# First pair's low halves by TensorE and ScalarE, and its maxima's turn and two scores placed ahead of the second pair's join and maxima

## The chip, the cores and the metric

The kernel runs on one core of one Trainium2 chip. Its time is device time in microseconds (us), median of the runs shown. The engines of the core work side by side, each through its own instructions in a fixed order: TensorE (PE in the profile; its weight loads are PEld), VectorE (DVE), ScalarE (ACT), GpSimd (POOL) and SyncE (SP), which issues all transfers of this kernel.

## The reference, cut to what matters

Attention with rotary positions, then a soft mixture of experts on its output:

```python
q_rot, k_rot = rotate(q), rotate(k)              # 8 batches, 8 heads, 576 positions, 64 wide
scores = (q_rot @ k_rot.T) / 8
attn = softmax(scores)                           # with the row's maximum taken off
x = (attn @ v) as 4608 x 512
logits = x @ phi                                 # 32 slots
d = softmax of logits over the 4608 rows;  c = softmax of logits over the 32 slots
slots = d.T @ x;  slots = relu(slots @ w1[e]) @ w2[e]   # 8 experts, 4 slots each
out = c @ slots
```

## The kernel before, in words

Heads are worked in 32 pairs, two heads a pair, one on each half of the 128 partitions. For a pair, q and k (`t` = 0 and 1) are loaded with their rotated partners (`load0`, `load1`), multiplied with cosine and sine (`spin0`, `spin1`, on POOL but for pair 0, which DVE does at the start), and added (`join`, DVE). The float32 result is then split: `high` (ACT) rounds it to fp16, and `low` (DVE, line 254) takes that off the float32 value and keeps the rest as fp16. So `halves[p]` holds four fp16 rows of 576: QL, QH, KH, KL. `low` is also the last reader of the loaded tile. There are two such tiles (`x_in`), so the load of pair p + 2 waits for `low` of pair p.

For the maxima of the scores there are eight units `m00` to `m31` (line 287) and `m_rem`: TensorE multiplies high halves, and DVE reduces the result to maxima. For pair 0, all units from the fourth on carry two extra matmuls that only keep TensorE at work (line 293). `m_min` joins the nine results. For pairs 0 and 1, `m_rows` is `m_lay` (line 343): float32 matmuls with the identity turn the maxima, and ACT writes them as fp16 to `peaks[p % 2]`. A score `t0` to `t8` (lines 360 and 376) is the sum of three products of halves and of a product with the peaks, and ACT takes its exponent from PSUM. `av0` to `av4` multiply with the values.

PSUM is cut in four buffers (`ps0` to `ps3`). `bank2()` gives the buffer that was freed longest ago, in the order of the program, or a named one, `bank2(k)`. A buffer has one copy: whoever gets it waits until every reader of the tile before has finished, also a reader that stands later in the program. `FIRST` turns the order in which the buffers are first given. Units, scores and turns take one buffer each in rotation; the accumulator of `av` keeps one from `av0` until it has been read.

PE, ACT and DVE each follow the order of the program. For the first part that order is the hand-written list `FRONT` (lines 87 to 110): names with pair numbers, such as `m11.0`. After it the events follow by due times. `heat` (line 720) issues matmuls whose result nobody reads. `id_sb`, the identity, is loaded at line 751, behind both loads of pair 1 and ahead of the values of pair 0. SP and POOL follow program order too.

After the last pair's `av4` (lines 787 to 802) the end of the attention runs: `natural` turns the outputs of pairs 29, 30 and 28 with nine transposes each (line 480), in named buffers; `norm_last` (line 458) lets DVE divide pair 31's accumulator straight from PSUM (lines 463 to 471); `natural_out` (line 500) copies the turned outputs by ACT; `natural_last` turns and copies pair 31; the logits of the last batch (line 506) take all four.

```python
    others = release_att()
    natural(last - 2, 2)
    natural(last - 1, 1)
    natural(last - 3, 0)
    norm_last(last)
    ...
    lt = bank2(2)
    ...                       # natural_last takes bank2(1) and bank2(3)
```

Then come the two layers of the experts (lines 903 and 927) and the combination (line 950) with the stores of the output.

Of the kernel before, what the change touches and what calls it, by code (L numbers as in the profile page):

```python
# [11 lines left out]
ALU = mybir.AluOpType  # L12
# [14 lines left out]
HC = S // 2  # L27
# [57 lines left out]
    3.879855, 5.365764), "bs3": 34.500363, "bs4": 35.968859, "bs5": 43.198227, "bs6": 50.043832,  # L85
}
FRONT = (
# [70 lines left out]
def attn_softmoe(ctx, tc, qk, v, phi, w1, w2, cs, ident, sel, seg, out):  # L158
    nc = tc.nc
    P = 128  # L160
# [23 lines left out]
    id_sb = const.tile([P, P], F32, name="id_sb")  # L184
# [9 lines left out]
    peaks = [const.tile([P, S], F16, name=f"peak{i}") for i in range(2)]  # L194
# [16 lines left out]
    loaded = {}  # L211
    halves = {}
    half = (slice(0, HC), slice(HC, S))
    parts = [slice(i, i + 1) for i in range(PIECE)]
    halves_q = (slice(0, PIECE // 2), slice(PIECE // 2, PIECE))
# [5 lines left out]
    def cut4(x):  # L221
        return x.rearrange("p (q w) -> p q w", w=PW)
# [23 lines left out]
    def high(p, t, c=every):  # L246
        if p not in halves:
            halves[p] = stk.tile([P, 4, S], F16, name="hl")
        out = cut4(halves[p][:, 1 + t, PW * c.start:PW * c.stop])
        nc.scalar.copy(out=out, in_=loaded[p][:, t, c, 0])  # L250

    def low(p):
        x, hl = loaded.pop(p), halves[p].rearrange("p t (q w) -> p t q w", w=PW)
        nc.vector.tensor_tensor(out=hl[:, 0:4:3], in0=x[:, :, :, 0], in1=hl[:, 1:3], op=ALU.subtract)  # L254
# [13 lines left out]
    def bank2(k=None):  # L268
        if k is None:
            k = min((i for i in range(N_S) if age[i] is not None), key=lambda i: age[i])  # L270
        age[k] = None
        t = ps[k].tile([P, 2, 512], F32, name=f"s_ps{k}")
        held[id(t)] = k, t
        return t

    def free(t):
        k, _ = held.pop(id(t))
        age[k] = next(ages)
# [397 lines left out]
    def part(k):  # L676
# [13 lines left out]
        "spin1": lambda p: spin(p, 1, nc.gpsimd, parts),  # L690
        "join": join,
        "high0": lambda p: high(p, 0),
        "high1": lambda p: high(p, 1),
        "low": low,
        "m_rem": m_rem,
# [24 lines left out]
    def heat(n):  # L720
        cold = bank2()
        free(cold)
        for _ in range(n):
            nc.tensor.matmul(cold[:, 0, 0:HC], lhsT=lift, rhs=halves[0][:, KH, 0:HC], start=True, stop=True)  # L724

    def small_loads(p):
# [1 line left out]
        nc.sync.dma_start(out=sel_sb, in_=sel)  # L728

    plan.update({  # L730
        "heat": lambda p: heat(16),
        "small_loads": small_loads,
        "join0": lambda p: join(p, 0),
        "join1": lambda p: join(p, 1),
# [1 line left out]
    done = set()  # L736
# [7 lines left out]
    for t, cc in ((1, 0), (1, 1), (0, 0), (0, 1)):  # L744
        c = halves_q[cc]
# [7 lines left out]
    for t in (1, 0):  # L753
        for c in halves_q:
            spin(0, t, nc.vector, (c,))
            join(0, t, c)
            high(0, t, c)
    done.update((n, 0) for n in ("spin0", "spin1", "join", "high0", "high1", "load0", "load1"))
    done.update((n, 1) for n in ("join0", "join1"))
    heat(N_WARM)  # L760

    last = NPAIR - 1
# [89 lines left out]
    for c in range(2):  # L852
        for j in range(4):
            nc.tensor.matmul(sh[c][32 * j:32 * j + 32], lhsT=dn[:, 32 * j:32 * j + 32],
                             rhs=xn[:, j, 256 * c:256 * c + 256], start=True, stop=True, tile_position=(0, 32 * j))
    for i in range(NP):
        nc.tensor.matmul(rp[32 * i:32 * i + 32], lhsT=dn[0:64, P + 32 * i:P + 32 * i + 32],
                         rhs=xn[0:64, 4, i * P:(i + 1) * P], start=True, stop=True, tile_position=(0, 32 * i))
# [31 lines left out]
    for _ in range(N_LEAD):  # L890
        load_w(wp, N_W)
    nc.vector.tensor_tensor(out=st[:, 0:256].rearrange("p (i e z) -> p i e z", i=NP, z=2 * SPE)[:, :, :, SPE:],
                            in0=fp[:, 0:P].rearrange("p (i e z) -> p i e z", i=NP, z=SPE),
# [173 lines left out]
```

## Time and profile before

| | us |
|---|---|
| median of 3 runs | 479.99 (479.64 to 480.94) |
| the profiled execution | 480.02 |
| its span | 478.2 |

| engine | busy us | share of the span |
|---|---|---|
| PE | 458.3 | 96% |
| PEld | 371.5 | 78% |
| DVE | 366.3 | 77% |
| POOL | 288.0 | 60% |
| ACT | 285.7 | 60% |

All times in the rows below are microseconds from the start of the span. A row of a timeline has start, length, engine, line of the kernel, operation, what it writes and reads, and in brackets how long the engine stood idle before it and what ended that. Consecutive instructions of one kind are merged in one row (x5). "PEclk" is the share of TensorE's full clock (2.4 GHz) that was granted; 0.50 is the other level, 1.2 GHz. 1.8 us of the execution lie outside the span.

### The profile page before, as it was taken

To read this page: it belongs to the slowest core of one execution; us is meant where nothing else is said; L and a number is where in the kernel's file an instruction comes from. 1 tells how busy PE (TensorE), PEld (TensorE's weight loads), DVE (VectorE), ACT (ScalarE), POOL (GpSimd) and SP (SyncE) were. 2 spreads that over 40 slices of the span, in tenths; PEclk is the share of its full clock that TensorE was granted. 3 is DMA by queue.
4 is the path that set the end of the run, shared out by engine and by line. 5 is a ranking of instruction groups with operands and counts; after the bars stand their busy time and mean duration, and the time that the engine had idled before them with its cause. 6 is when DMAs were issued, how large, how long until landed. Compare 5 with 4: busy or idle time off the path is not lost.

```text
span 478.2 us, 24158 instructions
## 1 busy us (share of the span) xinstructions
PE 458.3 (96%) x10787; PEld 371.5 (78%) x10787; DVE 366.3 (77%) x616; ACT 285.7 (60%) x656; POOL 288.0 (60%) x319
## 2 busy tenths in 40 slices
PE   4799999999999999999999999999999999989993
PEld 2487888878888888878887888888888888853762
DVE  5989998888878887998899789988896864263242
ACT  2156767675667567657765676577766766530242
POOL 4886958848783888488856886687749302120000
PEclk9899999999999999999999999999999999999998
DMA  7444845473655355446533653346352044799997
GB/s 280 172 166 176 269 153 197 164 261 102 202 175 213 110 201 174 120 145 210 171 113 123 250 172 125 149 139 217 126 191 112 15 181 163 237 382 407 408 370 319
DMA packets 28795, 93.97 MB, mean 196 GB/s; under 512 B 5012, under 2 KB 5396, under 8 KB 28692
## 3 DMA queue, kind: packets, MB, share of 16 engines
q1 hardware_dynamic: 28692, 92.44, 54.1%
q8 instruction: 84, 1.38, 1.2%
q14 instruction: 19, 0.16, 0.1%
HBM read 82.92 MB, written 9.44 MB: 193 GB/s over the span
## 4 chain that ended last, share of the span: by engine, by line
PE 91%; DVE 4%; ACT 2%; DMA 1%; issue 1%; SPq 0%; DVEq 0%; ACTq 0%
PE s_ps L407 33%; PE s_ps L372 26%; PE s_ps L296 8%; PE s_ps L387 4%; PE o_ps L927 3%; PE o_ps L903 3%; PE s_ps L480 2%; PE s_ps L517 2%; PE c_ps L950 2%; DVE nm L298 2%; PE s_ps L724 2%; PE s_ps L305 2%; PE s_ps L577 1%; DVE hl L254 1%; DMA x_in<-in_qk 1%
## 5 line engine op out<-in xcount | busy, mean ns | idle before, releaser
L237 POOL TENSOR_TENSOR x_in<-x_in,cs_sb 128x288 f32<-128x288 f32 x248 | 236.2, 986 | 79.5 <-DMA x_in<-in_qk 62.5
L298 DVE TENSOR_REDUCE nm<-s_ps 128x2 f32<-128x576 f32 x256 | 187.3, 752 | 50.0 <-PE s_ps L296 48.8
L407 PEld LDWEIGHTS s_ps<-v_in,a_t 128*64 128x64 f32 x4608 | 139.3, 137 | 12.4 <-issue 4.8
L373 ACT ACTIVATE a_t<-s_ps 128x576 f32<-128x576 f32 x256 | 146.0, 658 | 3.6 <-PE s_ps L372 3.1
L407 PE MATMUL s_ps<-v_in,a_t 128*64 128x66 f32 x4608 | 146.4, 222 | 0.2 <-issue 0.2
L372 PE MATMUL s_ps<-hl 64*128 64x288 f16 x1536 | 133.1, 283 | 0.4 <-DVE nm L307 0.2
L372 PEld LDWEIGHTS <-hl 64*128 64x128 f16 x1536 | 79.3, 94 | 18.5 <-issue 8.0
L372 PE MATMUL s_ps<-peak,lift 64*128 64x288 f16 x512 | 75.3, 283 | 0.3 <-ACT peak L349 0.3
L296 PE MATMUL s_ps<-hl 64*128 64x288 f16 x512 | 66.8, 286 | 0.7 <-ACT a_t L373 0.4
L438 ACT COPY o_sb<-s_ps 128x528 f32<-128x528 f32 x31 | 18.6, 601 | 74.9 <-PE s_ps L407 74.9
L456 POOL TENSOR_TENSOR xn<-o_sb,rr 128x640 f32<-128x640 f32 x31 | 41.0, 1332 | 31.7 <-PE s_ps L577 13.9
L254 DVE TENSOR_TENSOR hl<-x_in,hl 128x1152 f16<-128x1152 f32 x32 | 53.7, 1678 | 1.6 <-ACT hl L250 1.6
L250 ACT CAST hl<-x_in 128x576 f16<-128x576 f32 (+1 forms) x66 | 40.9, 659 | 20.5 <-DVE x_in L244 20.4
L244 DVE TENSOR_TENSOR x_in<-x_in 128x1152 f32<-128x1152 f32 (+1 forms) x35 | 46.2, 1321 | 0.1
L296 PEld LDWEIGHTS <-hl 64*128 64x128 f16 x512 | 29.0, 94 | 15.6 <-issue 6.8
L372 PEld LDWEIGHTS <-lift 64*128 64x128 f16 x512 | 27.0, 94 | 4.9 <-issue 0.5
L407 PE MATMUL s_ps<-v_in,a_tr 64*64 64x66 f32 x1152 | 26.4, 224 | 0.0
L307 DVE TENSOR_REDUCE nm<-s_ps 128x2 f32<-128x576 f32 x32 | 24.0, 749 | 2.5 <-PE s_ps L305 2.5
L407 PEld LDWEIGHTS s_ps<-v_in,a_tr 64*64 64x64 f32 x1152 | 21.9, 133 | 4.3 <-issue 3.5
L387 PE MATMUL s_ps<-hl 64*64 64x256 f16 (+1 forms) x384 | 23.9, 286 | 0.0
L962 DVE COPY w_exp<-c_ps 128x512 f32<-128x512 f32 x16 | 10.3, 686 | 17.3 <-PE c_ps L950 14.6
L500 ACT COPY xt<-s_ps 128x576 f32<-128x576 f32 x31 | 19.2, 650 | 5.0 <-PE s_ps L480 5.0
(174 smaller groups left out, 409.2 us busy)
## 6 DMA issues: line engine op xcount, KB each, us to landing
x_in<-in_qk SPq DMA_DIRECT2D x61, 576.0 KB
w_exp<-in_w SPq DMA_DIRECT2D x53, 512.0 KB
v_in<-in_v SPq DMA_DIRECT2D x32, 330.0 KB
out<-w_exp SPq DMA_DIRECT2D x18, 512.0 KB
wt<-in_w SPq DMA_DIRECT2D x11, 512.0 KB
peak<-mr SPq DMA_DIRECT2D x120, 0.5 KB
x_in<-in_qk SPq DMA_DIRECT2D x4, 288.0 KB
cs_sb<-in_cs SPq DMA_DIRECT2D x2, 288.0 KB
```

What stands on the lines that cost most here:

```text
L237: eng.tensor_tensor(out=run_on(x[:, c]), in0=run_on(x[:, c]), in1=run_on(cs_sb[:, c]), op=ALU.mult)
L244: nc.vector.tensor_tensor(out=x[:, :, 0], in0=x[:, :, 0], in1=x[:, :, 1], op=ALU.add)
L250: nc.scalar.copy(out=out, in_=loaded[p][:, t, c, 0])
L254: nc.vector.tensor_tensor(out=hl[:, 0:4:3], in0=x[:, :, :, 0], in1=hl[:, 1:3], op=ALU.subtract)
L296: nc.tensor.matmul(s[c, h, 0:HC], lhsT=hl[rows[h], QH, P * j + c.start:P * j + c.stop], rhs=hl[rows[h], KH, half[n]], start=True, stop=True)
L298: nc.vector.tensor_reduce(out=nm[:, n, j:8:4], in_=s[:, :, 0:HC], axis=AX.X, op=ALU.max, negate=True)
L307: nc.vector.tensor_reduce(out=nm[:, :, 8], in_=s[:, :, 0:HC], axis=AX.X, op=ALU.max, negate=True)
L372: nc.tensor.matmul(s[c, h, 0:HC], lhsT=lhs, rhs=rhs, start=(x == 0), stop=(x == 3))
L373: nc.scalar.activation(out=ats[p, b][:, :, half[n]], in_=s[:, :, 0:HC], func=AF.Exp, scale=SCALE)
L387: nc.tensor.matmul(s[rows[h ^ n], n, 0:w] if n else s[rows[h], 0, 512 - w:512], lhsT=lhs, rhs=rhs, start=(x == 0), stop=(x == 3))
L407: nc.tensor.matmul(o[rows[c], h, VW * u:VW * u + VW], lhsT=lhs, rhs=v, start=(i == 0 and u == 0), stop=(left_av[p] == 0 and u == 3 + (c == ...
L456: eng.tensor_tensor(out=xn, in0=t[:, :, :, 0:64], in1=rr.unsqueeze(3).broadcast_to([P, 2, 5, 64]), op=ALU.mult)
```

## The change

Pair 0's `low` leaves DVE. In its place `low_pe0` and `low_pe1` let TensorE form "float32 value times identity, plus high half times minus identity" in PSUM for q and for k, and ACT copies the result to the low half as fp16. The minus identity is an fp16 tile made once by DVE from `id_sb`, in the first columns of `peaks[1]`. In `FRONT`, the turn of pair 0's maxima (`m_rows.0`) and the scores `t5.0` and `t7.0` now stand ahead of `m30.1` and `m11.1`, the second pair's `join.1`, `high1.1` and `high0.1` stand behind `m_rows.0`, and `heat.0` issues 4 matmuls, not 16.

```diff
 FRONT = (
-    "logits.0 m11.0 m31.0 low.0 m00.0 spin0.1 spin1.1 m30.0 m20.0 m21.0 m10.0 join.1 m_rem.0 m01.0 load0.2 "
-    "high1.1 m_min.0 heat.0 high0.1 bs1.2 m30.1 m11.1 spin0.2 m_rows.0 low.1 t5.0 t7.0 weights.7 m31.1 t4.0 "
+    "logits.0 m11.0 m31.0 low_pe0.0 m00.0 spin0.1 spin1.1 m30.0 m20.0 low_pe1.0 m21.0 m10.0 m_rem.0 m01.0 load0.2 "
+    "m_min.0 heat.0 m_rows.0 join.1 high1.1 high0.1 bs1.2 t5.0 t7.0 m30.1 m11.1 spin0.2 low.1 weights.7 m31.1 t4.0 "
     "load_v.1 load1.2 t6.0 m20.1 t1.0 m21.1 spin1.2 load0.3 m10.1 join.2 t0.0 t3.0 load1.3 t2.0 m01.1 av0.0 m00.1 "
+    def low_pe(p, t):
+        hl, s = halves[p], bank2()
+        for n in range(2):
+            nc.tensor.matmul(s[:, n, 0:HC], lhsT=id_sb, rhs=loaded[p][:, t, halves_q[n], 0], start=True, stop=False)
+            nc.tensor.matmul(s[:, n, 0:HC], lhsT=minus, rhs=hl[:, 1 + t, half[n]], start=False, stop=True)
+        nc.scalar.copy(out=hl[:, 3 * t].rearrange("p (n c) -> p n c", n=2), in_=s[:, :, 0:HC])
+        free(s)
+        if t:
+            loaded.pop(p)
+
     plan.update({
-        "heat": lambda p: heat(16),
+        "low_pe0": lambda p: low_pe(p, 0),
+        "low_pe1": lambda p: low_pe(p, 1),
+        "heat": lambda p: heat(4),
     done.update((n, 1) for n in ("join0", "join1"))
+    done.add(("low", 0))
+    minus = peaks[1][:, 0:P]
+    nc.vector.tensor_scalar(out=minus, in0=id_sb, scalar1=-1.0, scalar2=0.0, op0=ALU.mult, op1=ALU.add)
     heat(N_WARM)
```

## Rows read from the trace of the kernel before

**Rows 1.** Page, chain that ended last: its shares by engine.

```profile
PE 91%; DVE 4%; ACT 2%; DMA 1%; issue 1%; SPq 0%; DVEq 0%; ACTq 0%
```

**Rows 2.** Stretches of the span: busy us of each engine (instructions), granted clock, DMA share, GB/s.

```profile
11.00:11.50 0.50, 0.46 (x4) 0.10 (x2) 0.06 (x1) 0.41 (x1) 0.50 (x1) 1.00 0.22 85
11.50:12.00 0.50, 0.42 (x8) 0.35 (x9) 0.50 (x1) 0.02 (x1) 0.50 (x2) 1.00 0.03 11
...
13.40:15.10 1.70, 0.00 (x0) 0.00 (x0) 1.70 (x3) 0.00 (x0) 1.70 (x2) 1.00 0.00 0
...
17.50:20.85 3.35, 3.35 (x17) 1.85 (x16) 3.08 (x6) 1.24 (x2) 2.28 (x3) 0.50 1.01 393
...
26.00:417.00 391.00, 389.82 (x9764) 330.27 (x9765) 322.84 (x527) 260.92 (x595) 266.66 (x277) 1.00 0.49 168
```

**Rows 3.** VectorE's timeline, 11 to 29 us.

```profile
11.50 1.42 DVE L298 TENSOR_REDUCE nm<-s_ps 128x2 f32<-128x576 f32 x2 [0.45 <-PE s_ps L296]
12.84 1.58 DVE L254 TENSOR_TENSOR hl<-x_in,hl 128x1152 f16<-128x1152 f32 x1
14.35 3.40 DVE L298 TENSOR_REDUCE nm<-s_ps 128x2 f32<-128x576 f32 x5
17.67 1.34 DVE L244 TENSOR_TENSOR x_in<-x_in 128x1152 f32<-128x1152 f32 x1
...
20.47 0.15 DVE L322 TENSOR_REDUCE cn_sb<-nm 128x2 f32<-128x4 f32 x1
21.15 1.42 DVE L298 TENSOR_REDUCE nm<-s_ps 128x2 f32<-128x576 f32 x2 [0.53 <-PE s_ps L296]
22.49 1.58 DVE L254 TENSOR_TENSOR hl<-x_in,hl 128x1152 f16<-128x1152 f32 x1
24.28 0.76 DVE L298 TENSOR_REDUCE nm<-s_ps 128x2 f32<-128x576 f32 x1 [0.21 <-PE s_ps L296]
...
27.38 1.35 DVE L244 TENSOR_TENSOR x_in<-x_in 128x1152 f32<-128x1152 f32 x1
```

**Rows 4.** TensorE's timeline, 17 to 29 us.

```profile
17.14 3.65 PE L724 MATMUL s_ps<-hl,lift 128*128 128x288 f16 x16 [0.24 <-DVE nm L298]
...
21.16 1.16 PE L346 MATMUL s_ps<-id_sb,cn_sb 128*128 128x128 f32 x8
...
25.16 0.55 PE L372 MATMUL s_ps<-hl 64*128 64x288 f16 x6
...
27.89 1.27 PE L407 MATMUL s_ps<-v_in,a_t 128*64 128x66 f32 x36
```

**Rows 5.** ScalarE's timeline, 19 to 27 us.

```profile
19.05 1.24 ACT L250 CAST hl<-x_in 128x576 f16<-128x576 f32 x2 [7.53 <-DVE x_in L244]
22.63 0.65 ACT L349 ACTIVATE peak<-s_ps 128x576 f16<-128x576 f32 x1 [2.34 <-PE s_ps L348]
23.66 2.86 ACT L373 ACTIVATE a_t<-s_ps 128x576 f32<-128x576 f32 x5 [0.39 <-PE s_ps L372]
```

**Rows 6.** Groups of TensorE instructions by line and shape: count, busy us, mean ns of one.

```profile
L903 PE MATMUL o_ps<-w_exp,peak 128*32 128x512 f32 x128 | 14.1, 594 | 0.3 <-DVE peak L892 0.3
```

**Rows 7.** Timelines of SyncE's queue and of GpSimd, 14 to 36 us.

```profile
14.45 0.33 SPq L232 DMA_DIRECT2D x_in<-in_qk  x1
...
18.57 7.66 POOL L237 TENSOR_TENSOR x_in<-x_in,cs_sb 128x288 f32<-128x288 f32 x8 [1.25 <-DMA x_in<-in_qk]
```

**Rows 8.** Timeline of all engines, 417 to 421 us.

```profile
417.20 1.29 PE L480 MATMUL s_ps<-id_sb,xn 64*128 64x64 f32 x27
417.76 1.72 ACT L500 COPY xt<-s_ps 128x576 f32<-128x576 f32 x3 [4.41 <-PE s_ps L480]
418.60 0.57 DVE L471 TENSOR_SCALAR xn<-s_ps,rr 64x64 f32<-64x64 f32 x2
418.99 0.69 PE L489 MATMUL s_ps<-id_sb,xn 64*128 64x64 f32 x9
```

**Rows 9.** Chain of waits from 406 us on: start, us, what.

```profile
427.05 10.51 PE o_ps L903 x96
```

## The prediction

> **What bounds the kernel now.** I read the chain of waits first: 91% of it is TensorE [rows 1]. The stretches show where that holds: from 26 to 417 us TensorE is busy 389.82 of 391.0 us [rows 2], so whatever delay TensorE carries at 26 us it still has at 417, and whatever it has gained it keeps. Two places are different, and the change touches both. At the start, from 11.5 us on, VectorE sets the pace: nine reductions of pair 0's maxima, with `low.0` and `join.1` between them [rows 3]. After 417 us TensorE, ScalarE and VectorE take turns in one chain [rows 8], and then TensorE alone runs the first layer of the experts [rows 9], so a delay there reaches the end too.
>
> I date the changed order by hand, instruction by instruction, with the durations of the rows. Times are from the start of the span.
>
> **The minus identity.** VectorE makes it before its first reduction, and the identity is the last transfer but one of the start. DMA falls from 85 to 11 GB/s around 11.5 us [rows 2], so it lands between 11.0 and 12.0; I take 11.4. The operation itself (128x128) has no row. It lies between 0.15 (a tiny reduction) and 0.76 us (one over 576 columns) [rows 3]; I take 0.2, near the small one, since it goes over 128 columns. Behind it stands the first reduction, which could start at 11.50 [rows 3] and now starts at 11.6. Bounds of this term: 0 to 1.1 us.
>
> **`low.0` becomes `low_pe0` and `low_pe1`.** VectorE loses an operation of 1.58 us (12.84) [rows 3]. TensorE gains, for each, two float32 matmuls of 288 columns and two of fp16. For float32: 128 instructions of 512 columns are 64 matmuls, four at a time in the array, so 16 steps in 14.1 us, 0.88 each [rows 6]; for 288 columns that is 0.50. The other row, the turn's four matmuls of 128 columns in 1.16 us [rows 4], would give up to 0.65. For fp16: 16 matmuls of 288 columns took 3.65 us at the granted 0.50 [rows 2, 4], 0.23 each, so 0.12 at full clock. A `low_pe` is then 2 x (0.50 + 0.12) = 1.24 us; the ends are 1.24 and 1.54 at full clock. ScalarE's copy out of PSUM is like `peak`'s, 0.65 us [rows 5], and ScalarE stands idle 7.53 us there [rows 5], so it is free except that its buffer goes back late.
>
> TensorE is in order, so the units behind wait. `m11` and `m31` reduce from 11.6 to 12.95. `low_pe0` runs from 11.85, when `m31`'s matmuls are through, to 13.1. `m00`'s result follows at 13.45: VectorE idles 0.5 us. `m00`, `m30`, `m20` reduce until 15.5 (a reduction starts 0.67 after the one before: five in 3.40 [rows 3]). `low_pe1` needs the buffer of `low_pe0`, copied by 13.9, so it runs 13.95 to 15.2, and `m21` behind it is ready to reduce at 15.65. Four reductions end at 18.35, and `m_min` at 18.65, where it was 20.62 [rows 3]. So 1.97 us earlier: 1.5 of `low.0` and 1.27 of `join.1` leave, 0.1 of minus identity and some 0.65 of new idle time come.
>
> **The queues it is moved past.** `load0.2` is issued when `low_pe1` has read the tile, 15.3 and not 14.45 [rows 7], and SP's queue is in order, so the weights, values and `load1.2` behind it move by 0.9 too. POOL's eight multiplications of pair 2 then end at 27.1 rather than 26.23 [rows 7]; `join.2` comes at 28.2 below, so this is hidden with about 1 us to spare. `heat` loses 12 matmuls; in front of the turn it held TensorE until 20.79 [rows 4] against `m_min`'s 20.62, 0.17 us.
>
> **The turn first.** `m_lay` starts at 18.7 and, at 1.42 us (from 21.16 until `peak` can start at about 22.6 [rows 4, 5]), ends at 20.1; `peak` runs 20.15 to 20.8. That is 1.8 us earlier. But ScalarE's order is now `peak`, `high1.1`, `high0.1`, `t5`, `t7`. VectorE has `join.1` ready at 19.95, and the two casts must stand behind `peak`: 20.8 to 22.05 (1.24 [rows 5]). Before, they ran at 19.05, long ahead of need. So `m30.1` can start only at 22.1 and its reduction at 22.4, where it was 21.15 [rows 3]; VectorE idles from 19.95 to 22.4. Two reductions, then `low.1`: it ends at 25.3 instead of 24.07 [rows 3]. This is where the gain goes. `m31.1`'s reduction stands behind `low.1`, 25.25 to 25.95 instead of 24.28 to 25.04 [rows 3], and `t1` takes the buffer that `m31.1` gives back. The scores `t5`, `t7`, `t4`, `t6` are done early (`t5`'s exponent at 22.05, not 23.66 [rows 5]), and then TensorE waits, from about 24.4 to 26.0. `t1` starts at 26.0; it started at 25.16 in the trace before. From there on the order up to `av0.0` (27.89 [rows 4]) is as before, with one short wait for a buffer less, so it arrives 0.7 to 0.85 us late. I take 0.8. `load0.3`, which waits for `low.1`, goes 1.2 us later, again covered by VectorE's own delay at `join.3`.
>
> So the front costs +0.8 us. If `minus` were free and the new idle times before `m_min` gone (9 x 0.67 + 0.3 from 11.5), `m_min` would be at 17.85, `low.1` still 0.4 us late and `t1` level with before: the lower end is 0. With `low_pe` at 1.54 twice (+0.6) and the minus identity at its upper bound, which `m00`'s reduction feels with 0.5, it is +1.9.
>
> **The end of the attention.** Nothing in the diff names it, but two more buffers are taken before the rotation goes on. I counted the calls of `bank2` through the whole order: from `m31.1` on every tile lies two buffers further than before, since `FIRST` stays. The last pair's accumulator was in buffer 3; now it is in buffer 1. The last lines name their buffers: `natural(29)` 2, `natural(30)` 1, `natural(28)` 0. So `natural(30)` takes the buffer that `norm_last` still has to read. Before, the 27 transposes ran without a gap from 417.20, beside `norm_last` [rows 8]. Now the second nine wait until `norm_last`'s last operation ends at 419.17 [rows 8]. Behind them on TensorE stand `natural(28)`, the first logits, `natural_last` and the other logits, and ScalarE waits with its copies. Nine transposes take 0.43 us (1.29 / 3), so `natural(30)` ends at 419.65; its copy (three in 1.72, 0.57 each [rows 8]) at about 420.3 gives buffer 1 to `natural_last`, which starts at 420.4 instead of 418.99 [rows 8]: +1.4 us. Nothing covers it. The bounds: 0.9, if the copy goes quicker and `natural_last` starts in its other buffer, and 1.7.
>
> **Sum.** 480.02 (the profiled execution, 0.03 above the median of the runs) + 0.8 + 1.4 = 482.2 us.
>
> **The rivals.**
>
> *The clock falls once more.* TensorE ran at the granted 0.50 from 17.50 to 20.85, after standing still from 13.40 to 15.10 [rows 2]; before, the 16 matmuls of `heat` filled that stretch, and nothing of value ran in it. Now only four are left, and TensorE stands still near 17 to 18.7, near 25 and at 417.7 to 419.2. If the same 3.35 us at half the clock fall on scores or on the first layer of the experts (10.51 us of TensorE alone [rows 9]), half of them, 1.7 us, is lost: 483.9. The Trainium skill, "TensorE: Matmul & The Clock Gate", Part 1, says that the throttled level is the default and that activity releases it. By that rule the cut in `heat` speaks against the change; the trace agrees that a pause was followed by the low level, and no run here shows it after these pauses. What speaks against the rival: `low_pe` fills the pause of 13.4 to 15.1.
>
> *The end keeps its cover* (the count of buffers is wrong, or the wait is short): only the front's 0.8 is left, 480.8. For it speaks only that the wait shows in no trace yet.
>
> *The front keeps its gain.* Its place is `t1`: if `t1` doesn't wait for the reduction behind `low.1`, TensorE goes on from `t5`, whose exponent starts 1.6 us earlier (22.05 against 23.66 [rows 5]). The price is -1.6 us, and it decides from the point where `low.1` ends before about 22.5. With the end's +1.4 that gives 479.8, not slower than before. Against it stand the casts behind `peak`. With both this and the rival above, 478.4.
>
> That the low halves by TensorE come too late for `t5` is excluded: they are there at 16.0, and `t5` starts at 20.1.
>
> **How the numbers follow.** The forecast has 0.58, with its own range 480.9 to 483.6 (front 0 to +1.9 and end +0.9 to +1.7, which sum to 480.9 and 483.6); the clock 0.15; the end covered 0.12; the front's gain 0.10; both 0.05. About 0.3% (1.44 us) is what a measurement of this kernel tells from no change, so the bounds are 478.55 and 481.43. Faster is the last case alone, 0.05. Within: 0.12 + 0.10, and 0.06 for the forecast's low end, 0.28. Slower: 0.67. The range reaches from 480.3, which takes in the case of the covered end, to 484.0, which takes in the clock; it leaves out the two cases with the front's gain and the dearest falls of the clock.
>
> **What would show it.** `m_min` at about 18.6 and `peak` at 20.2; the casts of pair 1 behind `peak`, the first reduction of pair 1 at 22.4 and `low.1` until 25.3; a pause of TensorE of over 1 us before `t1`; `av0.0` at 28.6 to 28.75. At the end, TensorE idle after nine transposes until VectorE's line 471 is through, and `natural_last` over 3 us after the first transpose instead of 1.79. The prediction is wrong if `av0.0` comes before 27.9, if the 27 transposes stay together, or if a second stretch of half the clock lies on useful work.

## The result, and the profile after

The changed kernel takes 485.24 us (median of 14 runs, 482.62 to 490.84); the kernel before, on the same chip, 480.43 us. The ratio is 1.0099 (95% interval 1.008 to 1.0117): 4.8 us slower. The forecast was slower, by 2.2 us, with a range up to 484.0: the sign is right, the size is not. The profiled execution took 486.31 us, its span 484.5.

Line numbers of the changed kernel are higher than before by 10 behind `low_pe`, and by 15 from the experts on. First the page: its chain by engine, which answers to [rows 1], and the granted clock in 40 slices.

```profile
span 484.5 us, 24162 instructions
PEclk9999999999999999999999999999999999979997
PE 91%; DVE 3%; DMA 2%; issue 1%; ACT 1%; SPq 1%; DVEq 0%; ACTq 0%
```

The shares look as before, so the loss has to be dated in the timelines. VectorE's timeline, 11 to 29 us, answers to [rows 3]:

```profile
11.83 0.23 DVE L774 TENSOR_SCALAR peak<-id_sb 128x128 f16<-128x128 f32 x1 [1.27 <-DMA id_sb<-in_ident]
11.98 1.42 DVE L308 TENSOR_REDUCE nm<-s_ps 128x2 f32<-128x576 f32 x2
13.67 2.09 DVE L308 TENSOR_REDUCE nm<-s_ps 128x2 f32<-128x576 f32 x3 [0.28 <-PE s_ps L306]
16.00 1.43 DVE L308 TENSOR_REDUCE nm<-s_ps 128x2 f32<-128x576 f32 x2 [0.24 <-PE s_ps L306]
...
18.96 0.15 DVE L332 TENSOR_REDUCE cn_sb<-nm 128x2 f32<-128x4 f32 x1
19.04 1.36 DVE L244 TENSOR_TENSOR x_in<-x_in 128x1152 f32<-128x1152 f32 x1
22.80 1.42 DVE L308 TENSOR_REDUCE nm<-s_ps 128x2 f32<-128x576 f32 x2 [2.40 <-PE s_ps L306]
24.14 1.88 DVE L264 TENSOR_TENSOR hl<-x_in,hl 128x1152 f16<-128x1152 f32 x1
```

TensorE and ScalarE in the same stretch answer to [rows 4, 5]:

```profile
19.19 1.13 PE L356 MATMUL s_ps<-id_sb,cn_sb 128*128 128x128 f32 x8 [1.67 <-DVE cn_sb L332]
...
22.46 0.85 PE L306 MATMUL s_ps<-hl 64*128 64x288 f16 x6 [0.35 <-ACT hl L250]
...
26.75 0.54 PE L382 MATMUL s_ps<-hl 64*128 64x288 f16 x6 [1.92 <-DVE nm L308]
```

```profile
20.63 0.65 ACT L359 ACTIVATE peak<-s_ps 128x576 f16<-128x576 f32 x1 [4.34 <-PE s_ps L358]
21.17 1.23 ACT L250 CAST hl<-x_in 128x576 f16<-128x576 f32 x2
```

Read them together: `m_min` is through at 19.11, 1.5 us earlier than before. Then TensorE does the turn and two scores, the casts of pair 1 stand behind `peak`, and VectorE is idle for 2.40 us before it gets the first maxima of pair 1. `low.1` ends at 26.02, and TensorE pauses for 1.92 us in front of `t1`. `av0.0` started at 29.36, 1.47 behind [rows 4].

The end, TensorE and VectorE, answers to [rows 8]:

```profile
420.07 0.53 PE L490 MATMUL s_ps<-id_sb,xn 64*128 64x64 f32 x9
422.18 0.80 PE L490 MATMUL s_ps<-id_sb,xn 64*128 64x64 f32 x18 [1.59 <-DVE xn L481]
...
423.41 0.53 PE L499 MATMUL s_ps<-id_sb,xn 64*128 64x64 f32 x9
423.86 2.15 PE L516 MATMUL s_ps<-xt,phi_sb 128*32 128x128 f32 x48
...
433.35 1.07 PE L918 MATMUL o_ps<-w_exp,peak 128*32 128x512 f32 x8 [0.31 <-DVE peak L907]
```

The 27 transposes are torn apart: nine, then TensorE waits for `norm_last`'s last operation (L481), as forecast. `natural_last` starts 3.34 us after the first transpose instead of 1.79 [rows 8], +1.55. The first layer of the experts starts 6.30 us later than in [rows 9]. Three parts make this up. One is the delay up to the last copy of an `av` accumulator by ScalarE, 410.1 against 407.4 us in the two traces: 2.77 (1.47 of it at the first such copy). The second is the 1.55. The rest, 1.98, is the clock but for 0.10 that comes ahead of the first transpose; the stretches show it (columns as in [rows 2]):

```profile
417.00:423.60 6.60, 5.01 (x166) 4.58 (x163) 1.76 (x7) 1.53 (x3) 0.18 (x1) 1.00 0.77 238
423.60:430.50 6.90, 6.33 (x86) 4.62 (x88) 1.98 (x8) 2.86 (x14) 1.43 (x6) 0.51 0.95 379
```

From 423.6 to 430.5 us TensorE ran at the lower of its two levels (1.2 GHz).

### The profile page after: what moved, and what is told of

Its sections match the earlier page's. It is cut to its first block, busy times and chain, and to the rows that moved or that the text cites. A ratio compares the mean times of both kernels' runs of the same rounds, so it can differ in the third digit from the quotient of the medians.

```text
span 484.5 us, 24162 instructions
## 1 busy us (share of the span) xinstructions
PE 461.9 (95%) x10787; PEld 372.7 (77%) x10787; DVE 367.1 (76%) x616; ACT 287.2 (59%) x658; POOL 289.3 (60%) x319
## 3 DMA queue, kind: packets, MB, share of 16 engines
q8 instruction: 84, 1.38, 1.2%
## 4 chain that ended last, share of the span: by engine, by line
PE 91%; DVE 3%; DMA 2%; issue 1%; ACT 1%; SPq 1%; DVEq 0%; ACTq 0%
PE s_ps L417 34%; PE s_ps L382 26%; PE s_ps L306 8%; PE s_ps L397 4%; PE o_ps L942 3%; PE o_ps L918 3%; PE c_ps L965 2%; PE s_ps L490 2%; PE s_ps L527 2%; PE s_ps L315 2%; DMA id_sb<-in_ident 2%; PE s_ps L587 1%; DVE nm L308 1%; DVE x_in L244 1%; PE s_ps L516 1%
## 5 line engine op out<-in xcount | busy, mean ns | idle before, releaser
L264 DVE TENSOR_TENSOR hl<-x_in,hl 128x1152 f16<-128x1152 f32 x31 | 49.8, 1607 | 1.4 <-ACT hl L250 1.4
L244 DVE TENSOR_TENSOR x_in<-x_in 128x1152 f32<-128x1152 f32 (+1 forms) x35 | 50.5, 1442 | 0.1
```

Of the source, the lines that this page charges most:

```text
L244: nc.vector.tensor_tensor(out=x[:, :, 0], in0=x[:, :, 0], in1=x[:, :, 1], op=ALU.add)
```

## The experiments

Each kernel was timed in five rounds beside the kernel before, on the same chip. "Lag" is the start of the same ScalarE copy of an accumulator, or of the same instruction, against the trace before.

**1. The end alone.** The kernel before with its buffers turned by two.

```diff
-FIRST = 1
+FIRST = 3
```

> The kernel before with FIRST = 3 alone: every PSUM buffer lies two further, nothing else differs. Theory (two costs: the front, and the last pair's accumulator in the buffer that natural(30) names): the front is as before, and at the end TensorE pauses after nine transposes until VectorE is through with pair 31; natural_last starts 1.4 to 1.6 us later against the first transpose. +1.5 us where the clock stays at full, +3.4 us where it falls behind the pause: median +1.5 to +3.4, 482 to 484 us. Rival (all of the loss comes from the start, the end only shows it): no difference, 480.4.

482.56 us, ratio 1.0051 (1.0032 to 1.0069). TensorE at the end of the attention:

```profile
416.85 0.52 PE L480 MATMUL s_ps<-id_sb,xn 64*128 64x64 f32 x9
418.96 0.81 PE L480 MATMUL s_ps<-id_sb,xn 64*128 64x64 f32 x18 [1.59 <-DVE xn L471]
420.19 0.52 PE L489 MATMUL s_ps<-id_sb,xn 64*128 64x64 f32 x9
```

3.34 us again, with nothing of the change but its side effect on the buffers. So the end term is shown. Its size is 1.55 in the trace and 2.4 in the medians. The lag at the last copy is -0.11, but at the first one it is +0.82, though the front is the same program: the lower clock held there from 14.9 to 21.7 us, before from 17.5 to 20.85 [rows 2]. A lag at the first copy, taken from one trace, is no better than that.

**2. The change without it.** The same edit in the changed kernel.

> The change with FIRST = 3: the end finds its buffers where the kernel before had them. Theory: no pause among the 27 transposes, no fall of the clock behind them, the front's delay stays: av0.0 of the first pair at 29.4 us instead of 27.9, the end 2 to 2.8 us late, 482.4 to 483.2 us. Rival (all from the start): as the change, 485.2.

481.92 us, 1.0041 (1.0026 to 1.0056). The 27 transposes are together again (418.13 to 419.43), `natural_last` 1.80 after the first of them. VectorE still stands idle in front of pair 1:

```profile
22.80 1.42 DVE L308 TENSOR_REDUCE nm<-s_ps 128x2 f32<-128x576 f32 x2 [2.59 <-PE s_ps L306]
```

Without the end the change costs 1.96 us by the ratio; the forecast had +0.8 for it. In this trace, the fastest of the ten runs, it is 0.94 at the first copy and 0.96 at the last. With the end (0.51%) that makes 0.92%, the change's 0.99% within the intervals.

**3. The pause at the end filled**, so that TensorE doesn't rest before the second nine transposes.

```diff
+    cold = bank2()
+    free(cold)
+    fill(cold[:, 0, 0:P], 26)
     natural(last - 1, 1)
```

> The change with 26 matmuls of 128 columns that nobody reads, put on TensorE after the first nine transposes of the end, where it pauses for 1.6 us. Theory: the pause lets the clock fall to its lower level for 6.8 us over the experts' start, which cost 1.9 us in the profiled execution; filled, the clock stays, natural_last comes no earlier, and the median falls by up to 1.9 us, to about 483.5. Rival (the clock falls for the pauses after it as well, or the fall belongs to the profiled execution alone): 485.2.

485.85 us, 1.0152 (1.0109 to 1.0194). Two of the six runs took over 490 us, the others 485.2 to 486.2, so the median didn't fall: the theory missed. The profiled execution is the slowest of the six (491.31). In it the pause was filled, and the clock fell later:

```profile
420.51 1.63 PE L434 MATMUL s_ps<-lift 128*128 128x128 f16 x26
```

```profile
430.00:440.00 10.00, 9.85 (x68) 5.13 (x70) 5.76 (x20) 1.30 (x6) 2.46 (x6) 0.56 0.68 254
```

But ahead of this fall TensorE stopped once more, for a reason that the profile doesn't name:

```profile
429.18 0.48 PE L852 MATMUL t_ps<-id_sb,m_run 128*128 128x128 f32 x1 [2.85 <-issue]
```

So this execution doesn't show a fall without a pause. The run isn't clean either: it has 26 more matrix products on TensorE, and experiment 12 shows that a count like that can cost time by itself.

**4. The order alone**: the new `FRONT`, with `low.0` left on VectorE and `heat` 4.

```diff
-"... m20.0 m21.0 m10.0 join.1 m_rem.0 m01.0 load0.2 "
-"high1.1 m_min.0 heat.0 high0.1 bs1.2 m30.1 m11.1 spin0.2 m_rows.0 low.1 t5.0 t7.0 ..."
+"... m20.0 m21.0 m10.0 m_rem.0 m01.0 load0.2 "
+"m_min.0 heat.0 m_rows.0 join.1 high1.1 high0.1 bs1.2 t5.0 t7.0 m30.1 m11.1 spin0.2 low.1 ..."
```

> The order of the change with low.0 left on VectorE and without the minus identity; heat 4; no buffer is turned. Theory (the second pair's casts behind the turn cost more than the turn gains): m_min at 19.3 instead of 20.6, the casts behind peak end at 22.8, first reduction of pair 1 at 23.1 instead of 21.15, low.1 done 1.9 us later; +1.5 to +2 us, 482 us. Rival (the loss of the front is TensorE's extra work and the wait for the identity; the order itself gains what join.1 cost): -1.3 us, 479.1.

483.95 us, 1.0079 (1.0055 to 1.0103). VectorE and then TensorE:

```profile
24.13 1.42 DVE L298 TENSOR_REDUCE nm<-s_ps 128x2 f32<-128x576 f32 x2 [3.26 <-PE s_ps L296]
```

```profile
19.27 2.04 PE L346 MATMUL s_ps<-id_sb,cn_sb 128*128 128x128 f32 x8 [1.67 <-issue]
```

The order loses; the rival that it gains falls. But the turn ran at half the clock here (2.04 us instead of 1.13), so the size is not the order's own: see experiment 14.

**5. The low halves alone**: `low_pe` in the old order (the minus lines of experiment 4 with `low_pe0.0` and `low_pe1.0` where the change has them), `heat` 16, `FIRST = 3`.

> The change's low halves by TensorE and ScalarE in the OLD order of the front (join.1 and high1.1 ahead of m_min.0, high0.1 behind heat.0, m_rows.0 behind spin0.2, t5.0 and t7.0 behind low.1, heat 16), buffers turned to FIRST = 3 so that the end keeps its cover. Theory (the order is the loss, the low halves gain): VectorE is freed of low.0 (1.58 us) and pays about 0.3 us for the identity, m_min.0 ends at 19.3 instead of 20.62, the first reduction of the second pair ends some 1.2 us earlier than before (21.15), av0.0 starts at 26.7 instead of 27.89; time 478.9, ratio 0.997. Rival (the low halves on TensorE cost as much as they free, since TensorE and ScalarE then end last): av0.0 at 27.6 to 28.4, time 480 to 480.6, ratio 1.000 to 1.001.

482.04 us, 1.0035 (1.0019 to 1.0051). The front gains, the first reduction of pair 1 starts at 20.46 instead of 21.15 [rows 3], the lag is -0.54 at 38 us and +0.13 at 407 us, and still the kernel is slower. The trace shows the loss behind everything: the last 38 us are 1.9 us longer.

**6. The identity first**: experiment 2 with the identity's load ahead of pair 1's two.

```diff
+    nc.sync.dma_start(out=id_sb, in_=ident)
     run("load0", 1)
     run("load1", 1)
-    nc.sync.dma_start(out=id_sb, in_=ident)
```

> The change with FIRST = 3 and the 64 KB load of the identity put ahead of the second pair's two loads. Theory (the wait for the identity is a small part of the front's loss): VectorE's wait for it (0.40 us with the same kernel otherwise) goes, m_min.0 ends 0.3 us earlier, everything behind the second pair's first maxima moves by 0 to 0.3; time 481.6 to 481.9, ratio 1.0035 to 1.004. Rival (the identity's late landing is most of the loss that was not foreseen): the lag behind the kernel before at av0.0 falls from +0.94 by 0.6 or more; time 481.0 or less, ratio 1.002.

481.17 us, 1.0028 (1.0009 to 1.0048). The wait for it is gone; the lag at 38 us is +0.88 against +0.94. A small part, if any.

**7. The casts ahead of `peak`**: experiment 2 with `join.1` ahead of `m_rem.0` and `high1.1 high0.1` ahead of `m_min.0`; the turn stays ahead of `m30.1`.

> The change with FIRST = 3, but join.1 back ahead of m_rem.0 and both casts of the second pair (high1.1, high0.1) ahead of m_min.0; the turn and the two scores t5.0 and t7.0 stay ahead of m30.1. Theory (the loss is the casts standing behind the turn's peak on ScalarE, so the second pair's maxima start late): the casts end at about 19, join.1 delays m_min.0 by its 1.3 us to about 20.2, the first reduction of the second pair is done within 0.5 us of that of the kernel before (21.15) in place of 22.80, av0.0 within 0.5 us of 27.89; time 479.7 to 480.4, ratio 0.999 to 1.001. Rival (it is the turn and the two scores ahead of the second pair's units that cost, wherever the casts stand): the first reduction at 22.3 or later, time 481.3 to 482, ratio 1.003 to 1.004.

484.79 us, 1.0087 (1.0065 to 1.0108). The rival holds: TensorE, then VectorE:

```profile
21.01 2.05 PE L356 MATMUL s_ps<-id_sb,cn_sb 128*128 128x128 f32 x8 [2.86 <-DVE cn_sb L332]
```

```profile
25.87 1.43 DVE L308 TENSOR_REDUCE nm<-s_ps 128x2 f32<-128x576 f32 x2 [4.95 <-PE s_ps L306]
```

The casts were done at 20.6, and the first reduction of pair 1 still came 4.7 us later than before, behind a turn and two scores at half the clock. The size is not to be compared with the change, whose front ran at full clock. What costs there can be read from the change's own trace: TensorE was through with `t7` at 22.12 us and waited for the casts only 0.35 us more (22.46, above). So it is mainly the work ahead of pair 1's units that keeps VectorE waiting; the casts add at most 0.35.

**8. The change again**, unaltered.

> The change itself, unaltered, for a second profile. Theory (the two further losses of the first profile in the middle, 0.57 us at 38 to 50 us and 0.86 at 321 to 333 us, are of that execution): the lag behind the kernel before is +1.2 to +2 at 407 us and stays flat from 60 us on; natural_last again 3.34 us behind the first transpose; time 484 to 485, ratio 1.009. Rival (they belong to the change): the lag steps up again between 321 and 333 us by 0.5 or more and is +2.7 at 407 us; time 485 to 486. The half clock at the end: if it is set by the pause of TensorE in front of the second nine transposes, it comes again from about 423.6 us on for some 7 us; if not, it is missing or elsewhere.

485.06 us, 1.0087 (1.0062 to 1.0113): the time repeats. `natural_last` came 3.35 us after the first transpose. The lag was +2.09 at 38 us. The step between 321 and 333 us did not recur, but steps of 1.4 (162 to 185 us) and 1.0 (396 to 407) did, so the lag at 407 us was +4.42, above both forecasts: losses of this kind move from execution to execution. The half clock at the end was missing:

```profile
423.60:430.50 6.90, 5.46 (x124) 4.17 (x124) 2.11 (x9) 3.74 (x15) 1.29 (x5) 1.00 0.94 354
```

The same pause (1.60 us) stood in front of it, and in experiment 1 too (1.59 us), where the clock at the end did not fall either: one fall in three traces. The pause alone doesn't decide it.

**9. Experiment 5 again.**

> The kernel of the run with the low halves by TensorE in the old order, unaltered, for a second profile. In its first profile the front was ahead of the kernel before by 0.54 us at 38 us, even with it at 407 us, and the last 30 us were 1.9 us longer (0.4 in the second matrix product, 1.5 behind the last copy to the output's buffer). Theory (the long end is of that execution): last VectorE instruction to the end of the span takes 6.5 us again as in the kernel before, span 478 to 479, and more runs move the median towards 480.5 to 481.5, ratio 1.001 to 1.0025. Rival (TensorE's low halves cost time that the front does not show): the median stays at 482, ratio 1.0035, and the second profile shows a loss of 1 us or more behind 50 us as well.

482.93 us, 1.0063 (1.004 to 1.0087). The median is the rival's. The trace puts 1.5 us of the loss at the same place as in 5, behind everything, and the lag grew by 1.28 between 38 and 407 us, 0.79 of it behind 61 us: the rival forecast such a loss, of 1 us or more.

**10. Experiment 5 with the identity first** (the edit of 6).

> Low halves by TensorE in the old order, FIRST = 3, and the identity loaded ahead of the second pair's two loads. Theory (the wait of 0.4 us for the identity is on VectorE's chain, which bounds the front in this order): m_min.0 and the second pair's first reduction end 0.3 to 0.4 us earlier against the end of the first pair's last join than with the late identity; time 0.3 less than that kernel's, 481.7 if that stays at 482. Rival (it is off the path): no change of the distance, 482.

482.37 us, 1.0039 (1.0019 to 1.006). In front it is the best so far, 0.79 us ahead of before at 38 us (experiment 5: 0.54; 9: 0.14); the medians don't resolve that. The long end is there a third time.

**11. The turn behind pair 1's units again**, `join.1` and the casts left behind `m_min.0` (experiment 2 with `... bs1.2 m30.1 m11.1 spin0.2 m_rows.0 low.1 t5.0 t7.0 ...`).

> The change with FIRST = 3, join.1 and the casts of the second pair behind m_min.0 as in the change, but the turn of the first pair's maxima (m_rows.0) back behind spin0.2 and its two scores t5.0 and t7.0 back behind low.1, so that the second pair's units m30.1 and m11.1 go first on TensorE. Theory (the front's loss is VectorE without work for 2.4 to 2.6 us while TensorE does the turn and two scores): the idle time in front of the second pair's first reduction falls from 2.59 us to 1.2 or less (join's end to cast's end to first unit), av0.0 at 27.8 to 28.3 instead of 28.83, time 480.6 to 481.3, ratio 1.001 to 1.002. Rival (it is join and casts behind m_min.0 that cost): idle stays above 2 us, time 481.9 or more, ratio 1.004.

483.53 us, 1.0072 (1.0048 to 1.0096). The theory missed; the rival has the time right (481.9 or more) but not the idle time. VectorE's idle time fell to 1.80 only, and TensorE, with four products of `heat`, then had nothing until the casts:

```profile
22.10 0.66 PE L306 MATMUL s_ps<-hl 64*128 64x288 f16 x4 [4.22 <-ACT hl L250]
```

By the stretches it ran at half the clock from about 20.8 to 27.6 us. So the order's moves hang together: `join.1` behind `m_min.0` takes away what TensorE would do, unless the turn fills it.

**12. Twelve instructions.** The ends of 5, 9 and 10 share a number: TensorE has 12 matrix products more than before. Here the kernel before gets 12 more, and next to no more work: one warming product of 288 columns becomes 13 of 24 (312 columns).

```diff
-    heat(N_WARM)
+    cold = bank2()
+    free(cold)
+    for c in [24] * 13 + [HC] * (N_WARM - 1):
+        nc.tensor.matmul(cold[:, 0, 0:c], lhsT=lift, rhs=halves[0][:, KH, 0:c], start=True, stop=True)
```

> The kernel before with one of its 21 warming matrix products of 288 columns split into 13 of 24 columns: 12 instructions more on TensorE ahead of everything, as many as the low halves in the old order add, the same columns, nothing else. Theory (the long end of the three profiles of the low halves in the old order is a piece of TensorE's instructions more, the 85th of 16,384 bytes, loaded while SyncE issues the last pieces of the output): an 85th piece is loaded in the last 10 us, the issue of an output piece at its side takes about 2.1 us instead of 0.45, the span is 1.5 us longer: 481.6, ratio 1.003. Rival (it belongs to the low halves or to that execution): the end is 6.5 us behind the last VectorE copy as before, 480.1, ratio 1.000.

482.73 us, 1.0053 (1.0036 to 1.007). The pieces of TensorE's instructions loaded (queue q8: count, MB) and the issue of an output piece by SyncE, in the kernel before:

```profile
q8 instruction: 84, 1.38, 1.2%
```

```profile
470.67 0.45 SPq L963 DMA_DIRECT2D out<-w_exp  x1
```

and with twelve more:

```profile
q8 instruction: 85, 1.39, 1.2%
```

```profile
470.91 2.03 SPq L966 DMA_DIRECT2D out<-w_exp  x1
```

An 85th piece is loaded 9.4 us before the end, and the issue beside it takes 2.03 us. From the start of that issue to the end of the span are 9.10 us instead of 7.57: 1.53, as in 5 (9.11), 9 (9.09) and 10 (9.02). So the low halves were charged with a loading step of TensorE's instructions. That twelve instructions lengthen the end is shown; that it is the load beside the issue which does it is read from these four traces. By the ratio the twelve cost 2.5 us, and about 1 us of that stays unexplained. Experiment 3 has an 85th piece too; there the load took 0.88 us and the issue beside it 0.33, so how the one holds up the other stays open. The Trainium skill, "Runtime: NRT & Kernel Launch", section "Instruction fetch mechanics", has blocks of 16 KiB and calls the cost of crossing one mostly hidden. The trace agrees on the size (16,384 bytes each); this one was not hidden.

**13. The low halves, lean.** Experiment 10 without the ten filler products between pair 0's units, which `low_pe` makes needless, and with two fewer in `heat`: as many instructions as before.

```diff
-N_COLD = 3
+N_COLD = 9
-        "heat": lambda p: heat(16),
+        "heat": lambda p: heat(14),
```

> Low halves by TensorE in the old order, FIRST = 3, identity first, and the ten filler products between the first pair's units left out (they keep TensorE busy where the low halves do so now), two fewer in heat: as many TensorE instructions as before. Theory (the front's gain is there, and the end's loss is the 85th piece): 84 pieces, the end 6.5 us again, VectorE no longer waits for TensorE between the first pair's units (0.34 and 0.25 us in the run with the identity early), the o_out copy at 38 us 0.8 to 1.3 us ahead of the kernel before; time 479.5 to 480.5, ratio 0.999 to 1.001. Rival (the gain in front is lost again by 61 us whatever its size, and further on): ratio 1.002 or more with 84 pieces and an end of 6.5 us.

479.57 us, 0.9982 (0.9968 to 0.9995): faster than the change, and just faster than the kernel before. 84 pieces again. The two waits of 0.34 and 0.25 us are gone, but VectorE waits once for 0.88 us instead. ScalarE's copies of the accumulators (first and last start), then VectorE:

```profile
L448 ACT COPY o_sb<-s_ps x31: 600/601/602, 36.6 to 407.7; 128x528 f32<-128x528 f32 x31
```

```profile
16.87 1.36 DVE L244 TENSOR_TENSOR x_in<-x_in 128x1152 f32<-128x1152 f32 x1
...
19.90 1.42 DVE L308 TENSOR_REDUCE nm<-s_ps 128x2 f32<-128x576 f32 x2
```

1.09 us ahead at 38 us. By 61 us 0.3 of it is lost, and in this execution a step of 1.0 between 311 and 333 us took the rest; the medians keep 0.9.

**14. The change's order, lean**: the change with `FIRST = 3`, the identity first and `N_COLD = 9`. From experiment 13 only the order and `heat` (4) differ.

> The change's own order of the front, with everything else mended as in the lean version of the old order: FIRST = 3, identity first, the ten filler products between the first pair's units left out; heat 4 as in the change. Against that lean version only the order of the front and heat differ. Theory (the change's order costs, by VectorE without work while TensorE does the turn and two scores before the second pair's units): m_min.0 at 18.3 or earlier, VectorE idle for 2.2 us or more in front of the second pair's first reduction, the o_out copy at 38 us 1.2 to 2.0 us behind that of the lean old order; time 480.8 to 481.6, ratio 1.0015 to 1.003. Rival (the order is worth its gain once TensorE isn't late): ratio 0.998 or less.

481.69 us, 1.0026 (1.0013 to 1.0038).

```profile
22.56 1.42 DVE L308 TENSOR_REDUCE nm<-s_ps 128x2 f32<-128x576 f32 x2 [2.40 <-PE s_ps L306]
```

```profile
L448 ACT COPY o_sb<-s_ps x31: 599/599/602, 38.6 to 411.3; 128x528 f32<-128x528 f32 x31
```

At full clock up to 29 us, and with `m_min` through at 18.86, it is 2.04 us behind experiment 13 at the first copy (+0.95 against -1.09), and 0.44% in the ratios, 2.1 us (give or take 0.9). That is the cost of the order with its shorter `heat`; the shorter `heat` was not run by itself.

## Why the forecast was right in sign and wrong in size

- **The end: right.** Counting the buffers told that `natural(30)` would wait for `norm_last`. Forecast +1.4, traces +1.55 (the change twice, and experiment 1); the medians have more, see below.
- **The front: right in kind, mis-sized.** The term was +0.8. The first trace has +1.47 at `av0.0`. Counted from the end of pair 0's last `join`, which moves between executions, the four traces with this front (the change twice, experiments 2 and 3) have 1.0 to 2.0, mean 1.5. Experiment 2's 1.96 by the ratio has the middle of the kernel in it. The identity landed at 11.8, not 11.4. A `low_pe` took 1.38 us (11.95 to 13.33), not 1.24. `m_min` was through at 19.11 instead of 18.65, the first reduction of pair 1 came at 22.80 instead of 22.4. `low.1` took 1.88 us where before it took 1.58, so it ended at 26.02 instead of 25.3, and `t1` at 26.75 instead of 26.0. The steps behind it were late by 0.4 to 0.75 each, in the order that was dated.
- **The reason inside it: half right.** I blamed the casts behind `peak`. They are late, but TensorE waited for them only 0.35 us longer than for its own turn and two scores, and experiment 7, with the casts early, still has pair 1's first reduction behind these. What costs is that TensorE does the turn and two scores while VectorE, which sets the pace there, has no maxima to reduce: 2.40 us idle. To put that work back is not enough (experiment 11), as `join.1` and the casts then come too late.
- **"Whatever delay TensorE carries at 26 us it still has at 417": wrong.** This is the step that failed: the sum has nothing for the middle of the kernel. Between the first and the last copy of an accumulator the lag grew by 1.30 us in the first trace and by 2.33 in the second. In all twelve traces with `low_pe` it grew (0.02 to 2.95, mean 1.4); without it, it changed by -0.93, -0.42 and +0.80 (experiments 1, 12 and 4). All this is against the one trace of the kernel before, which has a stop of 0.41 us of its own at 131 us; [rows 2] show one execution only.
  - 0.3 to 0.7 us of it come before 61 us in every kernel with `low_pe`; experiments 1, 4 and 12, without it, have -0.08, 0.00 and +0.22. In the first trace this part (0.57) lies at a score's matmuls between 39 and 41 us, beside a `join.3` of 1.93 us (1.35 before). Its cause was not tried.
  - The rest are steps that change place from execution to execution. The largest are stops of TensorE inside a run of `av` products, where the profile sees it wait for nothing. In experiment 8's trace two of them make 1.7 of the 2.33 us. Here is one of these, and one of experiment 14:

```profile
174.69 0.56 PE L417 MATMUL s_ps<-v_in,a_t 128*64 128x66 f32 x10 [0.90 <-issue]
```

```profile
134.22 0.98 PE L417 MATMUL s_ps<-v_in,a_t 128*64 128x66 f32 x27 [1.02 <-issue]
```

  Counted along all of TensorE's matrix products, these stops fall behind the same few numbers, whichever kernel it is: behind the 2,641st in the kernel before and in experiments 7, 9 and 14, behind the 7,609th in the first trace and in 11, 13 and 14, behind the 9,521st in 6 and 8. The 2,641st is not the same product in these kernels: of the `av` products it is number 1,498 before, 1,486 in experiment 9 and 1,508 in experiment 14. The numbers lie whole pieces of TensorE's instructions apart (one piece holds about 127.4 products with their weight loads), and each time TensorE went on 1.2 to 1.5 us after such a piece had landed; so did it after the 2.85 us of experiment 3. So it probably stood waiting for its own instructions. No run tried that, and why the kernels with `low_pe` lose more by it stays open.
- **The clock: the rival came half true.** It fell at the end in the first trace (1.98 us) but not in the second; it fell in front in experiments 2, 4, 7 and 11 and in the change's second trace (at 20.0 us). The forecast priced it as one event, 1.7 us; it can come at several places. In the first trace it was what the prediction named as a sign of being wrong, a second low stretch on useful work. In front it fell on useful work in five of the nine traces with `heat` 4, and in none of the four with `low_pe` and `heat` 14 or 16. The change with `heat` 16 was not run, so the share of the shorter `heat` is open.

The sum by medians: the order 2.1 (13 to 14), the end 2.4 (experiment 1) to 2.8 (the change less experiment 2), together 4.5 to 4.9 of 4.8. Each of these has an interval of some 0.9 us to both sides, so that they meet so well is partly luck. The low halves with their fillers come out at about nothing: experiment 10's 1.0039 less the 85th piece (1.53 us, 0.32%) is 1.0007; less all of experiment 12's 0.53% it is 0.9986. Lean, they gain 0.9 (experiment 13). In the change's order neither the early identity nor the missing fillers make up for it (experiments 6 and 14, 1.0028 and 1.0026). Open is why the end costs 0.9 to 1.3 us more in the medians than the 1.55 of the traces. The mean granted clock of experiment 1's runs is 0.987 against 0.992 of the runs before beside it, which fits; but in its trace the longer low stretch is the one in front (14.9 to 21.7 us), and nothing here separates it.

## What to carry to other kernels

Work moved forward on one engine is paid by the engine that waits for what now stands behind it: ask which engine sets the pace in the stretch, and don't put other work in front of what feeds it. Where buffers rotate, an edit that takes two more of them at the start changes who collides with whom at the far end; count the rotation through. Before a part of a change is judged by its time, look whether its instruction count alone moves a loading step: add the same number of empty instructions to the kernel before. Where a trace loses time without a wait, count how many instructions of that engine lie ahead of the place, and compare the count between kernels.

## What the runs showed of the hardware that was not expected

- Twelve small matrix products at 6 us made the end, 465 us later, 1.53 us longer: the 85th piece of TensorE's instructions came beside an output issue, which took 2.03 instead of 0.45 us.
- TensorE stopped for up to 1.02 us inside a run of products, behind the same numbers of instructions in different kernels, and went on 1.2 to 1.5 us after a piece of instructions had landed.
- VectorE's additions and subtractions over 1152 columns (`join` and `low`) took 1.31 to 2.46 us over the 16 traces. The Trainium skill, "SBUF — State Buffer", section "Who interferes with whom", has such an operation with two inputs in SBUF contend with GpSimd's reads. GpSimd was busy without a gap beside the 1.88 of `low.1`, and beside experiment 2's 1.35 too, so that alone doesn't decide it; no run here tells it apart.
- The start differs between executions: pair 0's last `join` on VectorE, behind the first transfers, began between 9.56 and 10.84 us and ended between 10.02 and 11.80 over the 16 traces, so a single trace doesn't date the front to better than that.
